# Single K, V, Q buffers, K transposed on TensorE, Q through the crossbar only from batch 2, operand sums spread over FFN1

## Chip, cores and metric

The kernel runs on one core of a Trainium2 chip. The metric is the device time of one execution in microseconds (us). Every experiment was timed on one chip in turn with the kernel before. A ratio is the mean time of one kernel's runs over that of the other's runs of the same rounds, so it is not quite the ratio of the medians quoted beside it. The kernel after was not timed again beside its variants: its two runs lie 1.4 us apart, and the kernel before, timed in every round, had medians from 559.58 to 560.78 us. Differences from the kernel after of under about 1.5 us therefore settle nothing.

Engines in the profile: PE is TensorE (PEld its weight loads), DVE is VectorE, ACT is ScalarE, POOL is GpSimd. SPq is the queue of the sync engine, which issues the output stores and the crossbar (DMA) transposes. L276 is line 276 of the kernel.

## The reference

```python
k_proj = einsum('ks,bhsd->bhkd', E, k)          # batch 8, heads 8, seq 1024, head_dim 64; E, F: 64 x 1024
v_proj = einsum('ks,bhsd->bhkd', F, v)
attn   = softmax(q @ k_proj.T / 8)              # 64 keys per head
x      = (attn @ v_proj), heads side by side    # 8192 x 512
out    = relu(x @ w_in)**2 @ w_out              # w_in 512 x 2048, w_out 2048 x 512
```

Everything is float32 at the interface.

## The kernel before

For each of eight batches the kernel runs the feed-forward part (FFN) of batch b. Between the FFN's steps it places pieces of the attention of batch b+1. The FFN of a batch has two chunks of 512 tokens. A chunk has 16 steps of FFN1 (each four matmuls of 128x512 into `ps_h`; relu on ScalarE; after every second one the square `hsq` on VectorE). Then come seven products of a Strassen-like scheme, which need the blocks of `hsq`, sums `s0..s3` of them, and combinations `T1..T4` of `w_out`. A11 and A12 are blocks of `hsq`; W11, W21 and so on are blocks of `w_out`. The first product that needs a sum (s0 by T1) goes into `ps_z`; its start is the mark from which this document measures a batch.

In the attention, `kp` and `vp` are the projections of K and V, `kT` and `qT` the transposes of `kp` and Q, `rs` the reciprocal of the row sums, and `xT` the attention's output, which the FFN reads.

```python
qkv_pool = tc.tile_pool(name="qkv", bufs=2)
def load(b): ...                      # K, V, Q of batch b, float32 -> bf16, issued by GpSimd

class Attention:
    def __init__(self, b, kvq):
        self.crossbar = b > 0
        ...
        if self.crossbar:
            nc.sync.dma_start_transpose(out=self.qT[:], in_=self.Q[:]...)
    def project(self): ...            # kp, vp from K, V; then, if crossbar:
        nc.sync.dma_start_transpose(out=self.kT[:], in_=self.kp[:]...)
    def scores(self, pr): ...         # TensorE: needs kT and qT; then exp on ScalarE
    def sums(self, g): ...            # row sums on TensorE; rs = exp(-ln(sum)) on ScalarE
    def values(self, g, e): ...       # TensorE, then xT = ps * rs on VectorE

BLOCKS = {1: 0, 12: 1, 18: 2, 22: 3, 30: 4, 36: 5, 40: 6}   # FFN step -> piece of the next batch
# 0: project   1: scores 0, 1   2: sums 0, values 0,0   3: values 0,1   4..6: the same of head group 1
...
cur.first_stages()                    # batch 0: all on TensorE
combine_weights()                     # T1..T4 on VectorE
```

TensorE's order is fixed by the program. A scheduler sets the order of the other engines. The traces show VectorE and ScalarE keeping to it. A case on ScalarE stands with the profile after.

The softmax here doesn't subtract the row's maximum and nothing guards it: scores larger than these inputs give would overflow.

## Time and profile before

| | before |
|---|---|
| time, median of 2 runs | 560.78 us (560.58 to 560.97) |
| TensorE busy | 481.8 us of a span of 558.2 us |
| TensorE waits for kT in all / longest | 30.2 us / 24.0 us |
| TensorE waits for hsq | 8.0 us |
| steady batch with / without a wait for kT | 60.9 / 59.2 us |

First the page of the kernel before: busy time per engine, then 40 slices of 14 us (busy tenths of TensorE, its granted clock in tenths, busy tenths of the DMA engines).

```profile
PE 481.8 (86%) x3512; PEld 291.3 (52%) x3512; DVE 326.9 (59%) x374; ACT 251.1 (45%) x401; POOL 30.9 (6%) x42
...
PE   1436704999999998999899999999999999999996
...
PEclk9999955999999999999999999999999999999999
DMA  9999998282936447372908284602041201001101
```

TensorE stands nearly idle in the sixth slice (70 to 84 us), with a granted clock of 5 tenths, while the DMA engines are busy for 9 tenths or more. The list of TensorE's waits (engine, line, what it waited for: us in total, times, longest) says for what it waited:

```profile
PE ps_att L202 <- DMA kT<-kp: 30.2, 5, 24.0
PE ps_att L202 <- DVE xT L232: 8.5, 1, 8.5
PE ps_y L298 <- DVE hsq L282: 8.0, 14, 0.9
PE ps_att L163 <- DMA K_sb<-in_k_dram: 5.5, 1, 5.5
```

The windows table gives the same by stage: first the long wait, then a steady batch with a kT wait, then one without. Columns: the stretch and its length, busy us (instructions) of PE, PEld, DVE, ACT and POOL, granted clock, DMA share, GB/s.

```profile
66.80:90.80 24.00, 0.00 (x0) 0.00 (x0) 3.22 (x4) 0.60 (x1) 0.00 (x0) 0.59 1.16 185
...
322.00:383.00 61.00, 58.47 (x438) 35.71 (x436) 39.58 (x45) 31.04 (x50) 1.75 (x2) 1.00 0.44 90
383.00:442.20 59.20, 58.05 (x435) 35.36 (x433) 39.58 (x45) 30.85 (x50) 0.00 (x0) 1.00 0.21 56
```

What the sync queue and GpSimd issued around that wait (two timelines of the kernel before; start, duration of the issue):

```profile
58.27 20.87 SPq L155 DMA_TRANSPOSE qT<-Q_sb  x1
79.20 3.28 SPq L177 DMA_TRANSPOSE kT<-kp  x1
...
111.61 5.62 SPq L155 DMA_TRANSPOSE qT<-Q_sb  x1
...
56.65 0.87 POOL L77 DMA_DIRECT2D K_sb<-in_k_dram  x1 [12.93 <-PE ps_att L163]
57.52 0.88 POOL L77 DMA_DIRECT2D V_sb<-in_v_dram  x1
```

Issuing the first Q transpose took 20.9 us instead of 5.6, and K's transpose was issued only after it, at 79.20 us. The time of the Q transposes from issue to landing (minimum/median/maximum over seven):

```profile
DMA to landing us min/median/max: 7.4/7.6/32.1
```

By these figures Q landed at 90.4 us (58.27 + 32.1). K landed at 90.8 us, and TensorE's wait ended there.

K's own transposes, over the seven batches:

```profile
DMA to landing us min/median/max: 2.6/9.6/11.6
```

The first took 11.6 us. The next four took 9.6 to 9.9 us, each issued within 1.1 us of a K and a V load (the first of them at 143.93 us, the loads at 142.85 and 143.72). The last two, at 387 and 446 us, had no such load beside them and landed in 2.6 us; these are the batches without a wait for kT.

### The profile page before, as it was taken

The numbers are of one execution on the slowest core, as the hardware profiler recorded it, in microseconds if no ns is written. First come the engines' busy times: TensorE is split into PE (matmuls) and PEld (weight loads), VectorE is DVE, ScalarE is ACT, GpSimd is POOL, SyncE is SP. The second block draws the span as 40 slices with busy tenths as digits, with TensorE's granted clock in tenths as the row PEclk, the third lists the DMA queues.
The fourth block names the chain that finished last, engine by engine and source line by source line (L and its number), as shares of the span: only waits on it lengthen the run. The fifth ranks groups of instructions, "written<-read, shape, count | busy, mean of one in ns | idle before, by whom it ended". The sixth has DMA issues, their size and how long they took to land.

```text
span 558.2 us, 8188 instructions
## 1 busy us (share of the span) xinstructions
PE 481.8 (86%) x3512; PEld 291.3 (52%) x3512; DVE 326.9 (59%) x374; ACT 251.1 (45%) x401; POOL 30.9 (6%) x42
## 2 busy tenths in 40 slices
PE   1436704999999998999899999999999999999996
PEld 0212302747365664647384746556564747474855
DVE  1224700576674858493766667484949385857482
ACT  0122503372556436462738255543745274726251
POOL 5230100000100010000000010000000000000000
PEclk9999955999999999999999999999999999999999
DMA  9999998282936447372908284602041201001101
GB/s 153 206 206 207 201 196 132 63 156 36 182 55 151 75 115 122 98 130 76 158 8 176 47 165 73 152 0 86 1 115 37 76 11 60 19 27 49 67 10 75
DMA packets 70852, 55.44 MB, mean 99 GB/s; under 512 B 33824, under 2 KB 62496, under 8 KB 70816
## 3 DMA queue, kind: packets, MB, share of 16 engines
q0 software_dynamic: 29248, 29.36, 33.3%
q1 hardware_dynamic: 41568, 25.56, 17.5%
q8 instruction: 27, 0.44, 0.3%
q14 instruction: 9, 0.07, 0.0%
HBM read 59.24 MB, written 16.78 MB: 136 GB/s over the span
## 4 chain that ended last, share of the span: by engine, by line
PE 63%; DMA 15%; DVE 13%; ACT 4%; SPq 2%; POOL 1%; issue 1%; POOLq 0%; DVEq 0%
PE ps_h L276 23%; PE ps_y L298 19%; PE ps_z L298 10%; DMA kT<-kp 9%; DVE hsq L282 6%; PE ps_x L298 5%; DMA w_in<-in_moe_w_in_dram 4%; DVE xT L232 3%; DVE s L288 3%; DMA w_out<-in_moe_w_out_dram 3%; SPq L155 2%; PE ps_att L163 2%; PE ps_att L202 2%; ACT rs L227 2%; ACT rs L226 1%; PE ps_att L216 1%
## 5 line engine op out<-in xcount | busy, mean ns | idle before, releaser
L276 PE MATMUL ps_h<-xT,w_in 128*128 128x512 bf16 x1024 | 231.8, 383 | 1.3 <-DVE xT L232 1.3
L282 DVE TENSOR_TENSOR hsq<-h_relu 128x1024 bf16<-128x1024 f32 x128 | 154.3, 1221 | 91.6 <-ACT h_relu L280 90.9
L280 ACT ACTIVATE h_relu<-ps_h 128x512 f32<-128x512 f32 x256 | 147.4, 600 | 74.8 <-PE ps_h L276 62.9
L276 PEld LDWEIGHTS <-w_in 128*128 128x128 bf16 x1024 | 97.8, 98 | 127.9 <-issue 18.6
L298 PEld LDWEIGHTS <-s 128*128 128x128 bf16 x1024 | 99.7, 98 | 13.0 <-issue 1.6
L298 PEld LDWEIGHTS <-hsq 128*128 128x128 bf16 x768 | 73.7, 98 | 27.4 <-DVE hsq L282 11.6
L298 PE MATMUL ps_y<-T,s 128*128 128x256 bf16 x512 | 62.3, 273 | 0.0
L207 ACT ACTIVATE expT<-ps_att 128x1024 bf16<-128x1024 f32 x32 | 31.3, 1026 | 46.2 <-PE ps_att L202 46.2
L379 ACT COPY o_sb<-ps_y 128x512 f32<-128x512 f32 x16 | 9.4, 585 | 89.5 <-PE ps_y L298 89.5
L202 PE MATMUL ps_att<-qT,kT 64*64 64x512 bf16 x128 | 11.8, 433 | 43.1 <-DMA kT<-kp 30.2
L232 DVE TENSOR_TENSOR xT<-ps_att,rs 128x1024 bf16<-128x1024 f32 x32 | 38.9, 1220 | 12.3 <-ACT rs L227 7.8
L298 PE MATMUL ps_y<-w_out,hsq 128*128 128x256 bf16 x256 | 35.7, 273 | 8.0 <-DVE hsq L282 8.0
L288 DVE TENSOR_TENSOR s<-hsq 128x1024 bf16<-128x1024 bf16 x64 | 42.0, 688 | 1.1
L361 DVE TENSOR_TENSOR o_sb<-ps_z,p_b 128x512 f32<-128x512 f32 x16 | 11.1, 692 | 40.4 <-PE ps_z L298 40.4
L298 PE MATMUL ps_x<-w_out,hsq 128*128 128x256 bf16 x256 | 33.2, 273 | 0.0
L298 PE MATMUL ps_z<-w_out,s 128*128 128x256 bf16 x256 | 30.6, 273 | 0.0
L298 PE MATMUL ps_z<-T,s 128*128 128x256 bf16 x256 | 30.6, 273 | 0.0
L298 PE MATMUL ps_y<-T,hsq 128*128 128x256 bf16 x256 | 30.5, 272 | 0.0
L168 DVE CAST kp<-ps_att 64x512 bf16<-64x512 f32 x8 | 5.5, 682 | 41.6 <-PE ps_att L164 41.6
L202 PEld LDWEIGHTS <-kT 64*64 64x64 bf16 x128 | 2.7, 109 | 49.0 <-DMA kT<-kp 32.7
L163 PE MATMUL ps_att<-K_sb,ET 128*64 128x512 bf16 x64 | 19.1, 445 | 5.5 <-DMA K_sb<-in_k_dram 5.5
L164 PE MATMUL ps_att<-V_sb,FT 128*64 128x512 bf16 x64 | 18.6, 444 | 4.4 <-DMA V_sb<-in_v_dram 4.4
(45 smaller groups left out, 236.5 us busy)
## 6 DMA issues: line engine op xcount, KB each, us to landing
out_dram<-o_sb SPq DMA_DIRECT2D x32, 512.0 KB, 2.8
K_sb<-in_k_dram POOLq DMA_DIRECT2D x8, 1024.0 KB, 11.0
V_sb<-in_v_dram POOLq DMA_DIRECT2D x8, 1024.0 KB, 15.2
Q_sb<-in_q_dram POOLq DMA_DIRECT2D x8, 1024.0 KB, 10.1
w_in<-in_moe_w_in_dram POOLq DMA_DIRECT2D x8, 256.0 KB, 19.7
w_out<-in_moe_w_out_dram POOLq DMA_DIRECT2D x4, 512.0 KB, 13.1
e_f<-in_E_dram SPq DMA_DIRECT2D x1, 256.0 KB, 3.6
e_f<-in_F_dram SPq DMA_DIRECT2D x1, 256.0 KB, 4.2
```

The costliest lines, as they stand in the source:

```text
L155: nc.sync.dma_start_transpose(out=self.qT[:], in_=self.Q[:].rearrange("p h c -> p (h c)"))
L163: nc.tensor.matmul(ps[0:KP, :], lhsT=ET[:, i, :], rhs=kv[:, :, i, :], start=f, stop=l)
L164: nc.tensor.matmul(ps[KP:P, :], lhsT=FT[:, i, :], rhs=vv[:, :, i, :], start=f, stop=l)
L202: nc.tensor.matmul(ps[o, bank, :], lhsT=self.kT[r, 2 * pr + j, :], start=True, stop=True, rhs=self.qT[r, NT * (2 * pr + j):NT * (2 * pr + ...
L207: nc.scalar.activation(e[:], ps[:], AF.Exp, scale=SCALE)
L227: nc.scalar.activation(rs[:], rs[:], AF.Exp, scale=-1.0)
L232: nc.vector.tensor_tensor(out=self.xT[:, 2 * g + e, :].rearrange("p (a t) -> p a t", a=2), in0=ps[:], in1=self.rs[g][:], op=ALU.mult,)
L276: nc.tensor.matmul(ps[:], lhsT=w_in_blk(cb, fb), rhs=xT[:, cb, ch * TCH:(ch + 1) * TCH], start=(cb == 0), stop=(cb == NCB - 1),)
L280: nc.scalar.activation(r[:, half], ps[:], AF.Relu)
L282: nc.vector.tensor_tensor(out=hsq[:, :, j, :], in0=r[:], in1=r[:], op=ALU.mult)
L288: tt = lambda o, x, y, op: nc.vector.tensor_tensor(out=o[:, js], in0=x, in1=y, op=op)
L298: nc.tensor.matmul(ps[:, tb * MH:(tb + 1) * MH], lhsT=lhs[:, j, tb * P:(tb + 1) * P], rhs=rhs[:, j], start=first and n == 0 and tb == 0, s ...
```

## The change

The intent is to take the crossbar transposes off the start, where loads fill the DMA engines (share 1.16 over the long wait); to let loads follow the projections; and to spread VectorE's sums so that squared blocks come in time. The core of the diff:

```diff
-    qkv_pool = ctx.enter_context(tc.tile_pool(name="qkv", bufs=2))
+    qkv_pool = ctx.enter_context(tc.tile_pool(name="qkv", bufs=1))
...
-            self.crossbar = b > 0
+            self.crossbar = b > 1
...
-            if self.crossbar:
-                nc.sync.dma_start_transpose(
-                    out=self.kT[:], in_=self.kp[:].rearrange("k h a d -> k (h a d)"))
...                                             # K: transpose_k() on TensorE, always
-    BLOCKS = {1: 0, 12: 1, 18: 2, 22: 3, 30: 4, 36: 5, 40: 6}
+    FROM_2 = {
+        8: [("project",)], 10: [("transpose_k",)], 14: [("scores", 0), ("scores", 1)],
+        18: [("sums", 0), ("values", 0, 0)], 22: [("values", 0, 1)],
+        32: [("scores", 2), ("scores", 3)], 38: [("sums", 1), ("values", 1, 0)], 42: [("values", 1, 1)],
+    }
+    BATCH_1 = {
+        31: [("project",)], 33: [("transpose_k",)], 35: [("transpose_q", 0)], 36: [("transpose_q", 1)],
+        37: [("transpose_q", 2)], 38: [("transpose_q", 3)], 40: [("scores", 0), ("scores", 1)],
+        43: [("sums", 0), ("values", 0, 0)], 46: [("values", 0, 1)],
+        49: [("scores", 2), ("scores", 3)], 52: [("sums", 1), ("values", 1, 0)], 55: [("values", 1, 1)],
+    }
...
-                if half and j % 4 == 3:
-                    sums(st["hsq"], st["s"], j // 4)
+                if half and 4 <= j < 7:
+                    sums(st["hsq"], st["s"], 0, (j - 4,))
+                if half and j == 7:
+                    sums(st["hsq"], st["s"], 0, (3,))
+                    sums(st["hsq"], st["s"], 1, range(4))
...
-            groups.extend([p1a, p1b, p2a])       # p2a: first half of A12*W21, then block 7 of A11*W11
+            groups.extend([p1a, p2a, p1b, p1c])  # p2a: first half of A12*W21; p1c: block 7 of A11*W11
```

Loads of batch b+2 are now asked for after batch b+1's last transposes in the program.

More of the change, by code (lines that the diff above doesn't have):

```diff
@@ L71, in ffn_psum, with load @@
         return fps.tile([P, 512], F32, tag="ffn", name=name)
-    def load(b):
-        tiles = []
-        for name, src in (("K_sb", k), ("V_sb", v), ("Q_sb", q)):
-            t = qkv_pool.tile([P, H, NI * D], BF16, name=name)
-            nc.gpsimd.dma_start(t[:], src[b].rearrange("h (p i) d -> p h (i d)", i=NI))
-            tiles.append(t)
-        return tiles
+    def load(name, src, b):
+        t = qkv_pool.tile([P, H, NI * D], BF16, name=name)
+        nc.gpsimd.dma_start(t[:], src[b].rearrange("h (p i) d -> p h (i d)", i=NI))
+        return t
     e_f32 = []
@@ L85 @@
         e_f32.append(t)
-    kvq = load(0)
+    first = [load(n, src, 0) for n, src in (("K_sb", k), ("V_sb", v), ("Q_sb", q))]
     nc.scalar.preload_act_table_set("natural_log_exp_and_others")
@@ L146, with __init__ @@
     class Attention:
-        def __init__(self, b, kvq):
-            self.K, self.V, self.Q = kvq
-            self.crossbar = b > 0
+        def __init__(self, b, K, V, Q):
+            self.b, self.K, self.V, self.Q = b, K, V, Q
+            self.crossbar = b > 1
             self.xT = x_pool.tile([P, NCB, 2 * TCH], BF16, name="xT")
@@ L155, in __init__, with following @@
                 nc.sync.dma_start_transpose(out=self.qT[:], in_=self.Q[:].rearrange("p h c -> p (h c)"))
+        def following(self):
+            b = self.b + 1
+            return [load(n, src, b) for n, src in (("K_sb", k), ("V_sb", v), ("Q_sb", q))]
         def project(self):
@@ L174, in project, with transpose_k @@
             nc.vector.tensor_copy(self.vp[0:KP], self.vp[KP:P])
+        def transpose_k(self):
             self.kT = proj_pool.tile([P, H, KP], BF16, name="kT")
-            if self.crossbar:
-                nc.sync.dma_start_transpose(
-                    out=self.kT[:], in_=self.kp[:].rearrange("k h a d -> k (h a d)"))
-        def transpose_k(self):
             ps = att_psum([P, H, KP], BF16)
@@ L249, in first_stages, with piece @@
                 self.values(g, 1)
-        def block(self, n):
+        def piece(self, name, n=0):
             with tc.high_priority(offset=400):
-                if n == 0:
-                    self.project()
-                else:
-                    g, n = (n - 1) // 3, (n - 1) % 3
-                    if n == 0:
-                        self.scores(2 * g)
-                        self.scores(2 * g + 1)
-                    elif n == 1:
-                        self.sums(g)
-                        self.values(g, 0)
-                    else:
-                        self.values(g, 1)
-    BLOCKS = {1: 0, 12: 1, 18: 2, 22: 3, 30: 4, 36: 5, 40: 6}
+                getattr(self, name)(*n)
+    FROM_2 = {
[9 more added lines that the diff above has]
+    }
     def ffn_groups(b, xT):
@@ L282, in first, with sums @@
                 nc.vector.tensor_tensor(out=hsq[:, :, j, :], in0=r[:], in1=r[:], op=ALU.mult)
-        def sums(hsq, s, q4):
+        def sums(hsq, s, q4, which):
             js = slice(4 * q4, 4 * q4 + 4)
@@ L287, in sums @@
             a12, a22 = hsq[:, 1, js, 0:TH], hsq[:, 1, js, TH:TCH]
-            tt = lambda o, x, y, op: nc.vector.tensor_tensor(out=o[:, js], in0=x, in1=y, op=op)
-            tt(s[0], a21, a22, ALU.add)
-            tt(s[1], s[0][:, js], a11, ALU.subtract)
-            tt(s[2], a11, a21, ALU.subtract)
-            tt(s[3], a12, s[1][:, js], ALU.subtract)
+            for o, x, y, op in (
+                (0, a21, a22, ALU.add), (1, s[0][:, js], a11, ALU.subtract),
+                (2, a11, a21, ALU.subtract), (3, a12, s[1][:, js], ALU.subtract),
+            ):
+                if o in which:
+                    nc.vector.tensor_tensor(out=s[o][:, js], in0=x, in1=y, op=op)
         def product(ps, lhs, rhs, js, first=False):
@@ L335, in p1a, with p2a, p1c @@
                 product(st["y"], st["A11"], W11, lo, True)
+            def p2a():
+                product(st["x"], st["A12"], W21, lo, True)
             def p1b():
                 product(st["y"], st["A11"], W11, range(4, 7))
-            def p2a():
-                product(st["x"], st["A12"], W21, lo, True)
+            def p1c():
                 product(st["y"], st["A11"], W11, range(7, 8))
@@ L392 @@
     with tc.manual_schedule(engines={PE}):
-        cur = Attention(0, kvq)
+        cur = Attention(0, *first)
         cur.first_stages()
         combine_weights()
+        loaded = cur.following()
         for b in range(B):
-            nxt = Attention(b + 1, load(b + 1)) if b + 1 < B else None
+            last = b + 1 == B
+            nxt = None if last else Attention(b + 1, *loaded)
+            pieces = {} if last else FROM_2 if b else BATCH_1
             for n, g in enumerate(ffn_groups(b, cur.xT)):
-                if nxt and n in BLOCKS:
-                    nxt.block(BLOCKS[n])
+                for name, *args in pieces.get(n, ()):
+                    nxt.piece(name, args)
+                    if name == ("transpose_q" if b == 0 else "transpose_k") and b + 2 < B and (b or args == [3]):
+                        loaded = nxt.following()
                 g()
```

## The prediction

> **What bounds it now.** TensorE is busy 481.8 of 558.2 us (busy table); its waits (list of waits) are 30.2 us for the crossbar transpose of K (scores waiting for kT), 8.0 us for squared activations before the A11·W11 product, and about 33 us of start-up. Of the 30.2 us, 24.0 us are one wait in batch 0 (67 to 91 us): the DMA engines are saturated with two batches of double-buffered loads, the Q transpose lands only 32.1 us after issue instead of 7.6 us, and the K transpose stands behind it on the same queue. Four more are about 1.4 us each. During the long wait the granted clock falls to 0.59, and to 0.77 in the 9 us after it (windows table). [...] Batch 1 needs 7.5 us from kT's arrival to the first ps_z product, batch 0 needs 9.6 us: 2.1 us lost to the cold clock. Steady batches last 60.9 us with the kT wait and 59.2 us without it.
>
> **What the change removes.** All kT waits (30.2 us) and the cold restart (2.1 us), because batch 1 needs no crossbar transpose, and K never does. Single-buffered loads (5 us apart for batch 0) have tens of us; later Q crossbar transposes (7.6 us) have half a batch.
>
> **What it adds.** Eight K transposes per batch, about 0.55 us of TensorE, seven times: 4 us. 32 Q transposes in batch 0, about 1.0 us per eight: 4 us. Each group ends with a VectorE copy (0.40 us for K, 0.69 us for Q). Lined up with VectorE's program order:
> - Batch 0, first half: no attention work left in it; its first ps_z product comes near 68 us instead of 100.4.
> - Batch 0, second half: all of batch 1's attention, about 36.5 us; batch 1 starts near 115 us instead of 140.
> - Batches 1 to 6, first half: the projection now stands at step 8, its two kp casts (1.35 us) queue behind hsq and s0, and the K transposes two steps later wait about 0.7 us.
> - Second half: scores and sums stand one step (0.86 us) later, VectorE waits in order for the row sums longer (1.6 us against 0.8), and hsq's last block comes late. I expect about 1.5 to 2 us of waiting for hsq against 1.2 us before.
>
> So a steady batch is about 60.8 us, against 59.2 to 60.9: over six batches a loss of some 3 us.
>
> **Sum.** 560.8 - 25 (batch 0, net of the Q transposes) + 3 = about 538 us, 4% faster. Range 530 to 546. Chances: faster by over 2% 0.94, within 2% 0.05, slower 0.01.
>
> **What would show it.** No wait for kT by DMA; the half-rate clock gone near 70 to 90 us; batch 0's two chunks about 26 and 36 to 37 us; the period of batches 1 to 6 between 60 and 61.5 us; waits of scores' K transposes on the kp cast 0.3 to 1 us each; waits for hsq between 6 and 16 us in total; TensorE busy up 7 to 9 us; VectorE busy up 5 to 6 us.
>
> **What would make it wrong.** A VectorE backlog worse than I lined up (batch 0's second half packs 9.75 us of attention beside the sums); the first Q crossbar transpose landing late for batch 2; or steady batches dropping to 59 us (then 528).

## The result, and the profile after

The kernel after takes 532.32 us (median of 2 runs, 531.6 to 533.03) against 560.78 us. The ratio is 0.949 (95% interval 0.944 to 0.955): 28.5 us or 5% faster.

The same views of the kernel after. The page first:

```profile
PE 483.9 (91%) x3600; PEld 292.5 (55%) x3600; DVE 328.6 (62%) x385; ACT 252.3 (47%) x401; POOL 30.8 (6%) x42
...
PE   1425999999999999999999999999999999999996
...
PEclk9855899999999999999999999999999999999999
DMA  9999309988482296625483295625560202020202
```

TensorE has no idle slice after start-up. Its waits, cut to three lines (lines have moved: L200 is the scores, L297 the products, L280 hsq, L230 xT, L171 the second kp cast, L181 the K transposes):

```profile
PE ps_att L200 <- DVE xT L230: 10.1, 1, 10.1
PE ps_y L297 <- DVE hsq L280: 6.8, 6, 1.1
...
PE ps_att L181 <- DVE kp L171: 1.1, 6, 0.2
```

No wait for kT by DMA is left. The windows table shows the stretch that was the wait, and a steady batch, which lasts 59.97 us from one batch's first ps_z product to the next one's (314.87 to 374.84 in the chain):

```profile
66.80:90.80 24.00, 24.00 (x205) 17.07 (x204) 15.02 (x21) 8.55 (x16) 1.75 (x2) 1.00 0.42 87
314.00:374.00 60.00, 58.69 (x442) 35.42 (x441) 39.47 (x47) 31.19 (x51) 2.62 (x3) 1.00 0.54 107
```

The Q transposes (six now) land evenly:

```profile
DMA to landing us min/median/max: 6.8/7.8/8.9
```

Where the time came from, by the start of a batch's first ps_z product in the chain of work that ended last:

| stretch | before | after | difference |
|---|---|---|---|
| start to batch 0's first ps_z product | 100.36 us | 71.00 us | -29.4 us |
| from there to batch 1's | 60.71 | 63.94 | +3.2 |
| from there to batch 7's (six batches) | 356.96 | 355.87 | -1.1 |
| from there to the end | 40.17 | 40.49 | +0.3 |
| span | 558.2 | 531.3 | -26.9 |

The profiled runs took 560.09 and 533.03 us, so they differ by 27.1 us and not by 28.5. Practically all of it comes from batch 0. The +3.2 us hold batch 1's projection and transposes, which now stand in batch 0's second half. The steady batches, to which most of the diff applies, give only 1.1 us in six batches.

In those batches the wait for kT is gone, which gains 0.7 to 1.1 us in each of the three that had one. The two that had none are 0.8 us longer than before (59.97 against 59.21). TensorE's wait for hsq is still 1.1 us a batch, now all of it in the second chunk. This is the chain in one of them (start, us, what):

```profile
391.70 0.60 ACT h_relu L278
392.30 0.92 ACT rs L224
...
393.25 1.06 ACT rs L225
...
394.33 1.22 DVE xT L230
395.56 2.27 DVE hsq L280 x2
397.82 1.14 DVE xT L230
398.96 0.60 DVE s L291
399.56 1.14 DVE hsq L280
...
403.03 1.14 DVE hsq L280
...
404.22 0.39 PE ps_y L297 x2
```

From 394 us on VectorE works without a pause, and TensorE waits for its last hsq. What happened just before is in the timeline of the same stretch (in square brackets: idle time before, and what ended it):

```profile
392.15 3.63 PE L274 MATMUL ps_h<-xT,w_in 128*128 128x512 bf16 x16
...
394.21 2.21 ACT L278 ACTIVATE h_relu<-ps_h 128x512 f32<-128x512 f32 x4
394.33 1.22 DVE L230 TENSOR_TENSOR xT<-ps_att,rs 128x1024 bf16<-128x1024 f32 x1 [1.64 <-ACT rs L225]
```

The next FFN1 step had its four matmuls (0.86 us) from 392.15 us on, but ScalarE could take its relu only at 394.21 us, after the two operations of `rs`. VectorE was idle for 1.64 us, and then had `xT` to do before the next hsq. In this trace ScalarE kept to the order of its queue: the relu, ready from about 393.0 us, stood 1.2 us behind `rs`, whose second operation began at 393.25 us, and ran at 394.21 us.

### The profile page after: what moved, and what is told of

Its sections match the earlier page's. It is cut to its first block, busy times and chain, and to the rows that moved or that the text cites. A ratio compares the mean times of both kernels' runs of the same rounds, so it can differ in the third digit from the quotient of the medians. Undisturbed runs are those within 1.5% of the kernel's fastest.

```text
span 531.3 us, 8368 instructions
## 1 busy us (share of the span) xinstructions
PE 483.9 (91%) x3600; PEld 292.5 (55%) x3600; DVE 328.6 (62%) x385; ACT 252.3 (47%) x401; POOL 30.8 (6%) x42
## 4 chain that ended last, share of the span: by engine, by line
PE 71%; DVE 15%; DMA 7%; ACT 4%; POOL 1%; issue 1%; POOLq 0%; DVEq 0%
PE ps_h L274 32%; PE ps_y L297 20%; PE ps_z L297 11%; DVE hsq L280 8%; PE ps_x L297 4%; DMA w_in<-in_moe_w_in_dram 4%; DVE xT L230 3%; DMA w_out<-in_moe_w_out_dram 3%; DVE s L291 3%; PE ps_att L200 2%; PE ps_att L214 1%; ACT rs L225 1%; ACT h_relu L278 1%; ACT rs L224 1%; DVE kp L171 1%; DVE kp L170 1%
## 5 line engine op out<-in xcount | busy, mean ns | idle before, releaser
L274 PE MATMUL ps_h<-xT,w_in 128*128 128x512 bf16 x1024 | 234.9, 383 | 1.3 <-DVE xT L230 1.3
L280 DVE TENSOR_TENSOR hsq<-h_relu 128x1024 bf16<-128x1024 f32 x128 | 154.9, 1220 | 86.9 <-ACT h_relu L278 86.9
L278 ACT ACTIVATE h_relu<-ps_h 128x512 f32<-128x512 f32 x256 | 149.3, 601 | 76.0 <-PE ps_h L274 73.8
L297 PEld LDWEIGHTS <-s 128*128 128x128 bf16 x1024 | 99.0, 98 | 14.6 <-issue 2.0
L297 PEld LDWEIGHTS <-hsq 128*128 128x128 bf16 x768 | 73.4, 98 | 25.8 <-DVE hsq L280 10.0
L297 PE MATMUL ps_y<-T,s 128*128 128x256 bf16 x512 | 61.2, 273 | 0.0
L230 DVE TENSOR_TENSOR xT<-ps_att,rs 128x1024 bf16<-128x1024 f32 x32 | 38.3, 1218 | 13.5 <-ACT rs L225 13.5
L297 PE MATMUL ps_y<-w_out,hsq 128*128 128x256 bf16 x256 | 35.2, 273 | 6.8 <-DVE hsq L280 6.8
L297 PE MATMUL ps_x<-w_out,hsq 128*128 128x256 bf16 x256 | 33.2, 273 | 0.0
L297 PE MATMUL ps_z<-T,s 128*128 128x256 bf16 x256 | 31.4, 273 | 0.0
L297 PE MATMUL ps_z<-w_out,s 128*128 128x256 bf16 x256 | 30.6, 273 | 0.0
L297 PE MATMUL ps_y<-T,hsq 128*128 128x256 bf16 x256 | 30.5, 272 | 0.0
L200 PE MATMUL ps_att<-qT,kT 64*64 64x512 bf16 x128 | 11.3, 418 | 14.4 <-DVE xT L230 10.1
L291 DVE TENSOR_TENSOR s<-hsq,s 128x1024 bf16<-128x1024 bf16 x32 | 22.0, 688 | 0.6
L348 ACT COPY p_a<-ps_y 128x512 f32<-128x512 f32 x16 | 9.3, 580 | 26.9 <-PE ps_y L297 26.9
L165 PE MATMUL ps_att<-K_sb,ET 128*64 128x512 bf16 x64 | 17.2, 413 | 5.1 <-DMA K_sb<-in_k_dram 5.1
L291 DVE TENSOR_TENSOR s<-s,hsq 128x1024 bf16<-128x1024 bf16 x32 | 21.8, 682 | 0.0
## 6 DMA issues: line engine op xcount, KB each, us to landing
Q_sb<-in_q_dram POOLq DMA_DIRECT2D x8, 1024.0 KB, 10.3
```

Source lines behind the costliest of these rows:

```text
L165: nc.tensor.matmul(ps[0:KP, :], lhsT=ET[:, i, :], rhs=kv[:, :, i, :], start=f, stop=l)
L200: nc.tensor.matmul(ps[o, bank, :], lhsT=self.kT[r, 2 * pr + j, :], start=True, stop=True, rhs=self.qT[r, NT * (2 * pr + j):NT * (2 * pr + ...
L230: nc.vector.tensor_tensor(out=self.xT[:, 2 * g + e, :].rearrange("p (a t) -> p a t", a=2), in0=ps[:], in1=self.rs[g][:], op=ALU.mult,)
L274: nc.tensor.matmul(ps[:], lhsT=w_in_blk(cb, fb), rhs=xT[:, cb, ch * TCH:(ch + 1) * TCH], start=(cb == 0), stop=(cb == NCB - 1),)
L278: nc.scalar.activation(r[:, half], ps[:], AF.Relu)
L280: nc.vector.tensor_tensor(out=hsq[:, :, j, :], in0=r[:], in1=r[:], op=ALU.mult)
```

## The experiments

Theory A: the gain is batch 0's, and comes from no longer transposing by DMA there. Two transposes stood one behind the other on one queue, the first of them slowed by loads. Rival B: double buffering, that is the collision of early loads with the transposes, is the whole cause. Rival C: the spread sums and the new product order give a good part.

| run | edit | median us | ratio to before (95%) | TensorE waits: kT / hsq / scores for xT at start |
|---|---|---|---|---|
| after | | 532.32 | 0.949 (0.944 to 0.955) | 0 / 6.8 / 10.1 |
| b1_single | before, single buffers only | 548.47 | 0.981 (0.976 to 0.986) | 18.5 / 8.1 / 8.5 |
| b2_batch1_pe | before, batch 1 transposed on TensorE only | 536.46 | 0.958 (0.956 to 0.960) | 5.9 / 8.1 / 9.1 |
| a1_double | after, double buffers | 532.79 | 0.951 (0.949 to 0.953) | 0 / 6.8 / 9.3 |
| a2_kcross | after, K by crossbar from batch 2, projection at step 1 | 530.10 | 0.947 (0.944 to 0.949) | 0.8 / 6.8 / 9.5 |
| a2b_kpe | after, projection at step 1 | 530.24 | 0.948 (0.945 to 0.950) | 0 / 6.8 / 9.3 |
| a3_sums_block | after, sums in blocks | 534.51 | 0.955 (0.953 to 0.957) | 0 / 10.3 / 9.6 |
| a4_old_order | after, old product order | 532.27 | 0.951 (0.949 to 0.954) | 0 / 6.7 / 9.5 |
| c1_late_T | after, T1..T4 later | 523.47 | 0.934 (0.932 to 0.936) | 0 / 6.9 / 1.7 |
| c2_early_g1 | after, second head group earlier | 522.46 | 0.933 (0.931 to 0.935) | 0 / 0 / 9.2 |
| c3_both | both | 513.39 | 0.916 (0.915 to 0.918) | 0 / 0.2 / 1.7 |
| c4_early_k | c3 and projection at step 1 | 512.10 | 0.914 (0.912 to 0.916) | 0 / 0.2 / 1.7 |
| c5_kcross | c4 and K by crossbar from batch 2 | 510.46 | 0.911 (0.909 to 0.913) | 0.7 / 0.2 / 1.7 |

All outputs are right. Median of 4 runs each (of 2 for after). In the fourth column 0 means that no such wait is listed.

### What made batch 0 slow: b1_single, b2_batch1_pe, a1_double

b1_single is the kernel before with `bufs=2` of the K, V, Q pool changed to `bufs=1`.

> The kernel before with single K, V, Q buffers and nothing else. Theory A (the 24.0 us wait comes from the two crossbar transposes standing one after the other in batch 0, made long by loads): K and V of batch 2 are still loaded right after batch 1's projection, so the Q transpose still shares the DMA engines for about 10 us, and the K transpose still stands behind it; the wait for kT shrinks to 8 to 14 us, time 545 to 551 us. Rival B (double buffering, that is load contention, is the whole cause): the wait falls under 3 us, time 536 us or less.

It took 548.47 us (548.10 to 553.96), a ratio of 0.981 (0.976 to 0.986). TensorE's waits for kT (the longest is that of batch 0), what the sync queue issued, and the landing of the Q transposes:

```profile
PE ps_att L202 <- DMA kT<-kp: 18.5, 6, 10.6
...
58.52 15.84 SPq L155 DMA_TRANSPOSE qT<-Q_sb  x1
74.41 1.25 SPq L177 DMA_TRANSPOSE kT<-kp  x1
...
DMA to landing us min/median/max: 7.4/7.8/18.0
```

The Q transpose now lands in 18.0 us instead of 32.1, the wait falls from 24.0 to 10.6 us, and the time by 11.3 us, as Theory A said. So rival B holds a part of the cause, but not all of it. K and V of batch 2 are loaded as soon as batch 1's projection has freed their buffers, and the two transposes still stand in line. Here too Q sets the end: it landed at 76.5 us (58.52 + 18.0), and K at 77.3 us, 2.9 us after its own issue.

b2_batch1_pe keeps double buffers and everything else of the kernel before:

```diff
-            self.crossbar = b > 0
+            self.crossbar = b > 1
...
+                if nxt and b == 0 and 3 <= n <= 7:
+                    with tc.high_priority(offset=400):
+                        if n == 3: nxt.transpose_k()
+                        else:      nxt.transpose_q(n - 4)
```

> The kernel before, double buffers kept, with only batch 1's K and Q transposes moved to TensorE (steps 3 to 7 of batch 0). Theory A: the 24.0 us wait and the 2.1 us of cold clock go, about 2.2 us of TensorE transposes come: 535 to 540 us, with the later kT waits of about 1.4 us each left. Rival B: the loads stay doubled, so much of the wait stays in another form (Q of batch 1 late): 545 us or more. Rival C (spread sums and product order give a good part of the gain): 540 us or more.

It took 536.46 us, 23.3 us less than the kernel before in the same rounds (559.81 us). The whole change with double buffers, the next run, gained 27.0 us in these rounds. Two lines of its wait list (the kT waits that stay are those of later batches):

```profile
PE ps_y L298 <- DVE hsq L282: 8.1, 14, 0.9
PE ps_att L202 <- DMA kT<-kp: 5.9, 4, 1.6
```

a1_double is the kernel after with `bufs=2` again.

> The kernel after with double K, V, Q buffers again. Theory A: no crossbar transpose runs while the early loads do, so the time stays within 1.5 us of the kernel after (531 to 534 us). Rival B: early loads collide again, 540 us or more.

It took 532.79 us, within the noise of the kernel after. Once no transpose runs beside the early loads, the number of buffers does not matter for the time. Theory A stands in this form: the cause is the DMA transposes beside the loads, and either side can be attacked. Taking the transposes away removes all of the wait; thinning the loads removes about half. No run moved Q's or K's transpose alone; by the landing times above Q's alone would have held TensorE until 90.4 us.

### What the rest of the change is worth: a2_kcross, a2b_kpe, a3_sums_block, a4_old_order

a2_kcross puts K's transpose back on the crossbar from batch 2 on, and a2b_kpe is its control:

```diff
# a2_kcross, in transpose_k(), and the place of the pieces
+            if self.crossbar:
+                nc.sync.dma_start_transpose(out=self.kT[:], in_=self.kp[:]...)
+                return
-        8: [("project",)], 10: [("transpose_k",)], 14: ...
+        1: [("project",), ("transpose_k",)], 14: ...
# a2b_kpe, the place only
+        1: [("project",)], 3: [("transpose_k",)], 14: ...
```

> The kernel after, but from batch 2 on K goes through the crossbar again, with the projection at step 1 and the first scores left at step 14. If K transposes on TensorE are needed for the steady batches: waits for kT of about 1.4 us per batch as before, 538 to 542 us. If they only cost (0.35 us of TensorE and 0.18 us of waiting for kp a batch) once scores stand two steps later: waits for kT under 0.3 us a batch, 528 to 531 us.

> Control of the run before it: projection at step 1 and K transposes on TensorE at step 3. The kp wait (0.18 us a batch, in six batches) goes or moves, K transposes stay: 531 to 533 us.

They took 530.10 and 530.24 us: no difference. K's transpose still takes 9.6 us to land (median of six). The scores stand two steps later than in the kernel before (14 against 12), and with that distance the crossbar is in time, but for one wait:

```profile
PE ps_att L204 <- DMA kT<-kp: 0.8, 1, 0.8
```

So K on TensorE did not itself win anything in the steady batches; the later place of the scores would have done. The control came out 0.8 us below its expectation. By its trace a steady batch lasts 59.7 us instead of 60.0.

a3_sums_block undoes the spreading:

```diff
-                if half and 4 <= j < 7:
-                    sums(st["hsq"], st["s"], 0, (j - 4,))
-                if half and j == 7:
-                    sums(st["hsq"], st["s"], 0, (3,))
-                    sums(st["hsq"], st["s"], 1, range(4))
+                if half and j % 4 == 3:
+                    sums(st["hsq"], st["s"], j // 4, range(4))
```

> The kernel after with the four operand sums again in one block at steps 4 and 8 of FFN1. If spreading them matters: hsq waits grow from 6.8 us to 9 to 14 us, time 535 to 539 us. Rival (VectorE reaches its last hsq at the same time either way, because the scheduler reorders): within 1 us of the kernel after.

It took 534.51 us: 2.2 us more than the kernel after, and also 2.2 us more than a4_old_order below in the same rounds, where no run of one (533.92 to 534.90 us) lies in the range of the other (532.13 to 533.71 us). That is just under the expected range; the hsq waits grew as expected:

```profile
PE ps_y L297 <- DVE hsq L280: 10.3, 12, 1.2
```

A steady batch in this trace lasts 60.47 us instead of 59.97. The spreading is worth about 2 to 3 us, a small part of the gain.

a4_old_order moves `product(x, A12, W21, lo)` from before blocks 4 to 6 of A11·W11 to behind them.

> The kernel after with the first half of A12.W21 moved back behind A11.W11's blocks 4 to 6. Its 0.87 us of work no longer covers the wait for hsq block 6, but stands after it and before block 7. If the last block sets the wait, nothing changes in the second halves (within 1 us); if block 6 does, the first halves and the second halves each wait some 0.2 to 0.8 us more: 534 to 540 us.

It took 532.27 us, and the hsq waits are 6.7 us in 12 pieces instead of 6.8 us in 6. The last block sets the wait, and the order of the products before it does not matter here. Rival C falls: of its two parts one gives 2 to 3 us, the other nothing.

### What still stood in the way: c1_late_T, c2_early_g1, c3_both, c4_early_k, c5_kcross

Two waits of the kernel after have the same form: VectorE stands, in order, before something that comes late, and work that TensorE needs is behind it. At the start T1, which needs w_out, stands ahead of xT, and the scores of the second head group wait for a PSUM buffer that this xT frees. In the steady batches the second head group's row sums (on ScalarE) and xT stand ahead of relu and hsq. c1_late_T makes T1 and T3 depend on the last xT of batch 0, by a copy of two columns that is overwritten at once, so that the scheduler can't put them first:

```diff
         cur.first_stages()
+        for t in (T1, T3):
+            nc.vector.tensor_copy(t[:, 0, 0:2], cur.xT[:, NCB - 1, 0:2])
         combine_weights()
```

> The kernel after, with two tiny copies that make the weight combinations depend on batch 0's last attention output, so that VectorE doesn't stand waiting for w_out (10.1 us wait of the scores at start-up). If that wait is on the path: batch 0's FFN starts 8 to 10 us sooner, 522 to 525 us. Rival: the next wait (w_in, w_out or K, V of batch 1) takes its place, under 3 us gained.

It took 523.47 us, 8.8 us less than the kernel after. The wait of the scores shrinks from 10.1 us to this:

```profile
PE ps_att L200 <- DVE xT L230: 1.7, 1, 1.7
```

T1 now starts at 43.80 us, and no wait of VectorE for w_out is listed any more.

c2_early_g1 moves the second head group of every next batch into the end of the first chunk, where VectorE has little to do:

```diff
-        32: [("scores", 2), ("scores", 3)], 38: [("sums", 1), ("values", 1, 0)], 42: [("values", 1, 1)],
+        25: [("scores", 2), ("scores", 3)], 28: [("sums", 1), ("values", 1, 0)], 30: [("values", 1, 1)],
```

> The kernel after, with the second head group of each next batch (scores, sums, values) at steps 25, 28 and 30 instead of 32, 38 and 42. If VectorE's in-order wait for the row sums (1.6 us a batch) makes the last hsq late: the hsq waits of 1.13 us a batch go (6.8 us in all to under 1), 525 to 527 us. Rival: hsq is late because VectorE has too much work in that half: within 2 us of the kernel after.

It took 522.46 us, 9.9 us less than the kernel after and 2.5 us below the lower end of what was expected. No wait for hsq is listed any more, and a steady batch lasts 58.34 us. The expectation had used the list of the matmuls' waits (6.8 us). The weight loads, which ran ahead of the matmuls (before the last hsq of the chain above the loads ended at 402.82 us, the matmuls at 403.09), waited longer; in the kernel after:

```profile
PEld L297 <- DVE hsq L280: 10.0, 12, 1.4
...
PE ps_y L297 <- DVE hsq L280: 6.8, 6, 1.1
```

The 10.0 us fit the gain of 9.9, but this agreement may be chance: in a3_sums_block both lists grew by about 3.5 us and the time by 2.2. By the windows table TensorE's idle time in a steady batch fell from 1.3 to 0.4 us, and its busy time from 58.67 to 57.95 us; why the busy time fell was not traced. VectorE's wait for the row sums is 13.5 us in the kernel after. In this run it is the line below, of which 2.4 us lie at the start, 1.3 us in batch 0 and 0.3 us in each later batch:

```profile
DVE xT L230 <- ACT rs L225: 5.4, 8, 2.4
```

The run does not separate the two theories as cleanly as intended. It takes the wait for the row sums out of the second chunk's FFN1, and also two xT (1.2 us each) of VectorE's work there. The place is shown to be the cause; whether the wait or the work weighs more stays open.

c3_both has both edits.

> Both of the two runs before it. If they are independent: 515 to 519 us.

It took 513.39 us: 18.9 us less than the kernel after, against 8.8 + 9.9 = 18.7 us for the two alone. Within the noise the two gains add up.

c4_early_k adds the placement of a2b_kpe, and c5_kcross adds K's crossbar transpose of a2_kcross to that.

> The fastest kernel so far (late weight combinations, second head group at steps 25, 28, 30) with the projection at step 1 and the K transposes at step 3. If the 2 us that this placement gave beside the kernel after add up: 510.5 to 512.5 us; if VectorE's work in the first half only shifts: 513 to 514 us.

> The same with K through the crossbar from batch 2 on. TensorE is spared 0.35 us a batch, six times: 2 us less than the run before it if the crossbar lands in time; 2 to 6 us more if scores wait for kT, as one did for 0.8 us in the earlier crossbar run.

They took 512.10 and 510.46 us. Neighbouring intervals touch or overlap, so neither single step of this pair is settled. c5_kcross is clear of c3_both (0.909 to 0.913 against 0.915 to 0.918) and is the fastest kernel: 50 us below the kernel before, 22 us below the kernel after.

## Why the prediction was right or wrong

The prediction was right: 532.3 us lies in the range of 530 to 546 us, and the direction was forecast with 0.94. It was 5.7 us too slow. Point by point:

- **The 24.0 us wait, and that it goes.** Right in mechanism, but for one part. The change took 29.4 us from the time to batch 0's first ps_z product. b1_single and b2_batch1_pe show that the wait is that for the DMA transposes beside the loads. The prediction also named K's place behind Q on the queue. By the landing times this added only 0.4 us to the wait (0.8 us in b1_single), because the scores need Q as well.
- **Single buffers do not hurt.** Right. a1_double shows that they do not help either.
- **First ps_z product near 68 us.** It came at 71.0 us (69.3 to 69.9 us in the profiles of a1_double, a3_sums_block and a4_old_order). The prediction left out that TensorE starts the FFN at half clock and stays there until 58 us (granted clock 0.51 from 52.3 to 58 us). In the start-up before it TensorE was busy for 15.9 of 49.4 us; no run shows whether that is the cause. By an estimate from the spacing of matmuls, 0.43 us there and 0.22 us later, the 13 FFN1 matmuls of this stretch cost 2.7 us more than later ones. In the kernel before the slow stretch ends at about the same time (57.5 us), but batch 1's projection fills most of it (its matmuls stand 0.42 us apart from 53.2 us on). It is a cost that did not go away, not a new one.
- **Q transposes at 1.0 us per eight, K transposes at 0.55 us.** Too large, and this was avoidable. Both sizes were read at start-up, where TensorE's matmuls stood twice as far apart. Two lines of the kernel before in start-up, then two of a steady batch (the K half of the projection):

```profile
17.98 0.63 PE L163 MATMUL ps_att<-K_sb,ET 128*64 128x512 bf16 x1
18.40 0.63 PE L163 MATMUL ps_att<-K_sb,ET 128*64 128x512 bf16 x1
...
384.16 0.38 PE L163 MATMUL ps_att<-K_sb,ET 128*64 128x512 bf16 x1
384.38 0.38 PE L163 MATMUL ps_att<-K_sb,ET 128*64 128x512 bf16 x1
```

  They start 0.42 us apart in start-up and 0.22 us apart later. In the kernel after, batch 1's Q transposes ran between matmuls 0.22 us apart, and eight took 0.45 us, read from the start of the next matmul:

```profile
86.36 0.61 PE L190 MATMUL ps_att<-ident,Q_sb 128*128 128x128 bf16 x8
86.81 1.03 PE L274 MATMUL ps_h<-xT,w_in 128*128 128x512 bf16 x4
```

  Eight K transposes took about 0.35 us (365.20 us to the next matmul at 365.54). So batch 0's second chunk took 33.9 us (80.6 to 114.5 us) instead of 36.5. This and the slow FFN start nearly cancelled: batch 1's FFN began at 114.5 us, predicted 115.
- **A steady batch of about 60.8 us.** This is the term that was mis-sized. It is 59.97 us, 0.8 us less, in five stretches (the sixth, in which no further batch is projected, lasts 56.0 us before and after). The prediction put a loss of 3 us on the six, and the table above shows a gain of 1.1 us: about 4 of the 5.7 us. The K transposes cost 0.2 us less. By the matmuls' list the wait for the kp cast was 0.18 us, not 0.7, and that for hsq 1.1 us, not 1.5 to 2. By the weight loads' list they were 0.7 and 1.7 us, much as predicted; it seems that the waits were there and TensorE felt less of them. Against a batch without a kT wait before, TensorE's busy time rose from 58.06 to 58.67 us and its idle time from 1.15 to 1.31 us. VectorE's wait for the row sums is 1.64 us, predicted 1.6, and c2_early_g1 shows that this group's place makes hsq late, by the wait, its work, or both. The predicted period of 60 to 61.5 us was just missed. The rest of the 5.7 us is batch 0 (26.2 us gained, predicted 25) and the difference between the profiled runs and the medians.
- **Busy times.** TensorE was to rise by 7 to 9 us and rose by 2.1; VectorE by 5 to 6 and rose by 1.7. TensorE's miss follows in part from the transposes' size (seven times 0.35 and four times 0.45 us are 4.3 us) and from the slow stretch after the wait in the kernel before (granted clock 0.76 from 90.8 to 100 us), in which busy time was stretched: the weight loads of the first FFN1 matmuls there started 0.43 us apart. VectorE's was not traced further. Records of operations that follow each other without a pause overlap (two hsq take 2.27 us together in the chain above, 1.22 us alone), so busy time does not simply add up.

## What to carry to other kernels

Here a DMA transpose that had to land while loads filled the DMA engines (share 1.16) took 32.1 us instead of 7.6. Even in the steady batches K's took 9.6 us beside loads and 2.6 us without. Keep such transposes out of the start-up, do those few on TensorE, or leave them the distance that they need; the buffer count is only the lever behind it. When a wait names the transfer that came last, look when the others that the consumer needs have landed. When an engine stands in order before a late input, as VectorE did here for 9.48 us, ask what is queued behind it: moving the late item, by two columns of false dependence or a few steps of placement, gave 18.9 us here after the large change had given 28.5. Read an operation's cost where it will run: at the start the projection's matmuls stood 0.42 us apart, and 0.22 us in the steady batches.

## Transposes and the clock's records, as measured

- By DMA, beside loads: the 1 MB Q transpose took 7.4 to 7.6 us from issue to landing in most batches of the kernel before, 32.1 us beside its first loads and 18.0 us beside those of b1_single. The loads came from GpSimd's queue and the transpose from the sync engine's. From 55 to 92 us of the kernel before, the first queue's packets took 90.4% and the second's 24.1% of the time of 16 DMA engines, so a queue of its own did not keep the transpose clear of the loads.
- On TensorE: one 128x128 bf16 transpose lasts 219 ns (median of 64 in the kernel after), but eight in a row between matmuls 0.22 us apart take 0.45 us of TensorE, 56 ns each, against about 120 ns each in the kernel before at start-up (22.65 to 23.61 us), where matmuls stood 0.42 us apart. A cost estimate needs this spacing.
- The clock's records: the kernel before records a granted clock of 1.00 from 0 to 49.1 us and the kernel after 0.74 from 0 to 49.4 us, while the projection's matmuls stand 0.42 us apart in both. In these two stretches the spacing of the matmuls is the better witness.
